# Last pair of batches: the second product of the second MLP in seven block products instead of eight

## The chip, the cores and the metric

One NeuronCore of a Trainium2 chip runs the whole program. The time is the device time of one execution in microseconds; the median of three runs of the kernel before is 1183.4 us (1183.0 to 1185.2).

## The reference

Attention with RMS-normed queries and keys (4 batches, 12 heads, 448 tokens, head size 64), then two MLPs on all 1792 tokens. The second one is what this change touches:

```
h = x @ w_in                       # 1792 x 768  @  768 x 2048
g = h * clip(h + 3, 0, 6) / 6
return g @ w_out                   # 1792 x 2048 @ 2048 x 768
```

## The kernel before

Everything is kept transposed: rows of the weights on the 128 partitions, the 448 tokens of a batch as the moving columns of a matmul. fp32 accuracy comes from splitting each operand into a high part (fp32r) and a low part (the rest), and from three matmuls for each product: high x high, high x low, low x high. A split is one ScalarE copy (the high part) and one subtraction on VectorE or POOL (the low part).

The second MLP works on pairs of batches: the first pair is batches 0 and 1, the last pair 2 and 3. Its work is a list of items (`items`, L1042), each of nine matmuls of 128 x 128 weights on 448 columns. Item i is handled in the main loop (L1219); six items ahead of it (`AHEAD2`) `prepare` (L1065) splits its weights (`halves`, L1004, which gives every second low part to POOL) into one of eight `wt` tiles.

*First product.* Two hidden blocks and two batches are a 2 x 2 block problem (the 768 inner rows are cut in halves), done by Winograd's form of Strassen's algorithm in seven products P1 to P7 instead of eight. The sums of weight blocks (S1 to S4, `temp`, L1078) are made by VectorE, the sums of the inputs beforehand by `xprep` (L1010). Two PSUM banks, sA and sB, take P1 + P6 + P7 + P4 and P2, then P5 + P3; the partial sums on the way are copied out or added (`strassen`, L1174), and the two banks change roles from one group of seven to the next (`swap`). So P2 of a group writes the bank that P4 of the group before has just used. `finish` (L1148) applies the nonlinear step (a ScalarE Relu and a VectorE minimum and product) and, for the pair's first batch, splits the result at once into a `g` tile (`gsplit`, L1143).

*Second product.* For the first batch of the pair, items "L" are woven into the first product's groups, two hidden blocks behind: one item is one hidden block times one half of the 768 outputs, three matmuls into each of three banks; six banks (`acc`) hold the 768 outputs. For the second batch, the hidden blocks wait in `G` tiles in SBUF, and after the groups a sweep of 32 items "M" goes over all of them. So a pair has 32 L items and 32 M items. Then the accumulators are copied out and stored (`out`, L1195).

*Weights.* Each weight tile that an item needs is a numbered use (`uses`, L924). `units` (L943) loads them in order into 12 `wf` tiles, most of them from the DRAM tensor `wfd`, where converted weights were put earlier; a tile is free again after `drop` (L977). All DMAs are issued on SP's queue, in order. Eight `u` tiles of one batch's width serve as temporaries (`utile`, L995).

*Order.* Program order is only a priority: a planner that walks the program with its own cost estimates gives each engine the first instruction that it holds ready, and that order is then fixed. `issue_after` keeps an instruction behind another one on the same engine.

Of the kernel before, what the change touches and what calls it, by code (L numbers as in the profile page):

```python
# [13 lines left out]
F32 = mybir.dt.float32  # L14
F32R = mybir.dt.float32r
# [12 lines left out]
P = 128  # L28
# [23 lines left out]
def fused_kernel(ctx: ExitStack, tc: tile.TileContext, nat, qT, kT, vin, gq, gk,  # L52
# [8 lines left out]
    x2d = dpool.tile([B, KD, P, S], F32, name="x2d")  # L61
    wfd = dpool.tile([2 * M2, P, DM], F32, name="wfd")
    wpd = dpool.tile([KD * M1 // 6, P, 6, 2 * P], F32, name="wpd")

    cpool = ctx.enter_context(tc.tile_pool(name="consts", bufs=1, side="left"))
    pp = ctx.enter_context(tc.tile_pool(name="psum", bufs=2, space=PSUM))
# [23 lines left out]
    def bank(tag, name="bank"):  # L90
        return pp.tile([P, 512], F32, tag=tag, name=name)
# [833 lines left out]
    for p in range(2):  # L925
        for j in range(M2 // 2):
            uses += [("in", 2 * j), ("in", 2 * j + 1)]
            if j:
                uses += [("out", 2 * j - 2), ("out", 2 * j - 1)]
        uses += [("out", M2 - 2), ("out", M2 - 1)]  # L930
        uses += [("out", q) for q in range(M2)]
    fresh = []
    for v, x in enumerate(uses):
        if x not in EARLY and x not in [uses[z] for z in fresh]:
            fresh.append(v)
    dropped = set()

# [5 lines left out]
    def units():  # L943
        n = 0
        for v, (kind, q) in enumerate(uses):
            while v >= NWF and v - NWF not in dropped:
                yield None
            t = mp.tile([P, DM], F32, tag="wf", bufs=NWF, name="wf")
            if v in fresh:
                n += 1  # L950
                load_raw(n)
                r = wr.pop(v)
                if r.dtype == F32:
                    nc.gpsimd.tensor_copy(t, r)
                    yield 0.9
                else:
                    yield from convert(t.bitcast(I32), r)
                yield 0.0
            else:
                dma(t, wfd[q + (M2 if kind == "out" else 0)])  # L960
                yield 0.0
            wf[v] = t

# [9 lines left out]
    def upto(v):  # L973
        while v not in wf:
            assert next(unit) is not None
# [13 lines left out]
    def store(v, t):  # L989
        kind, q = uses[v]  # L990
        dropped.add(v)
        with tc.issue_after(xo["last"].ins):
            dma(wfd[q + (M2 if kind == "out" else 0)], t)

    def utile():  # L995
        return mp.tile([P, S], F32, tag="u", bufs=8, name="u")
# [42 lines left out]

    ORDER = ("P1", "P2", "P6", "L0", "L1", "P5", "P7", "L2", "L3", "P3", "P4")  # L1040
    RIGHT = {"P1": "11", "P2": "21", "P6": "T2", "P5": "T1", "P7": "T3", "P3": "22", "P4": "T4"}
    items = []  # L1042
    base = 0
    for p in range(2):
        prev = None
        for j in range(M2 // 2):
            n = 4 if j else 2
            for z in ORDER:
                if z[0] == "P":
                    items.append((z, p, j, (base, base + 1), z == "P4"))  # L1050
                elif j:
                    h = int(z[1])
                    items.append(("L", p, 2 * j - 2 + h // 2, base + 2 + h // 2, h % 2))
            base += n
        for q in (M2 - 2, M2 - 1):
            for h in range(2):
                items.append(("L", p, q, base + q % 2, h))
        base += 2
        for q in range(M2):
            for h in range(2):  # L1060
                items.append(("M", p, q, base + q, h))
        base += M2
    wt, sx = {}, {}

    def prepare(i):  # L1065
        kind, p, j, v, h = items[i]
        if kind[0] != "P":
            upto(v)
            t = mp.tile([P, 2, NH], F32R, tag="wt", bufs=NWT, name="wt")
            wt[i] = halves(t, wf[v][:, h * NH : h * NH + NH])  # L1070
            if h:
# [23 lines left out]
        wt[i] = halves(t, src)  # L1095
        if h:
            drop(v[0])
            drop(v[1])
# [44 lines left out]
    def gsplit(p, b, q, src):  # L1143
        t = rp.tile([P, 2, S], F32R, tag="g", bufs=4, name="g")
        done[:] = [nc.scalar.activation(t[:, 0, :], src, AF.Copy), nc.vector.tensor_sub(t[:, 1, :], src, t[:, 0, :])]  # L1145
        g[p, b, q] = t

    def finish(p, j, z, src):  # L1148

        b, q = (z % 10 - 1), 2 * j + z // 10 - 1  # L1150
        if b == 0:
            _, u = nonlinear(src, None)
            gsplit(p, 0, q, u)
            return
        if (p, j) not in G:
            G[p, j] = rp.tile([P, 2, S], F32, tag="G", bufs=M2 // 2, name="G")
        nonlinear(src, G[p, j][:, q % 2])

    sA, sB = bank("s", "sA"), bank("s", "sB")
    swap = [(sA, sB)]  # L1160
# [34 lines left out]
    def out(n, t):  # L1195
        o = utile()
        if n % 2:
            nc.vector.tensor_copy(o, acc[n][:, :S])
        else:
            nc.scalar.activation(o, acc[n][:, :S], AF.Copy)  # L1200
        dma(outT[n * P : n * P + P, t * S : t * S + S], o)

    def layer4(i):
        kind, p, q, _, h = items[i]
        b = int(kind == "M")
        w = wt.pop(i)
        x = g[p, b, q] if h == 0 else g.pop((p, b, q))
        for n in range(3 * h, 3 * h + 3):
            if q == 0:
                acc[n] = bank(TAGS[1 + n // 2], "acc")  # L1210
            ns = slice(n % 3 * P, n % 3 * P + P)
            with tc.issue_after(snap["mm"].ins) if (kind, q) == ("L", M2 - 2) else ExitStack():
                mm3(acc[n][:, :S], w[:, 0, ns], w[:, 1, ns], x[:, 0, :], x[:, 1, :], q == 0, q == M2 - 1)
            if q == M2 - 1:
                out(n, PAIRS[p][b])

    prep_to(AHEAD2)
    xg = xrest(0)
    for i, it in enumerate(items):  # L1219
        if i == 4:  # L1220
            xo["last"] = L["last"]
            for e in kept:
                store(*e)
        prep_to(i + AHEAD2)
        kind, p, q = it[:3]
        with ExitStack() as es:
            if kind == "M":
                for z in done:
                    es.enter_context(tc.issue_after(z.ins))
# [12 lines left out]
        (strassen if kind[0] == "P" else layer4)(i)  # L1242
    d1.close()


# [44 lines left out]
```

## Time and profile before

| | |
|---|---|
| runs, median (lowest to highest) | 1183.4 us (1183.0 to 1185.2) |
| profiled execution | 1181.6 us, span 1179.8 us |
| mean granted TensorE clock | 0.994 |
| TensorE matmuls | 1140.6 us busy, 97% of the span, 5627 instructions |
| VectorE, ScalarE, POOL | 72%, 65%, 29% of the span |

The span goes from the first to the last instruction. The second MLP's items begin at about 731 us; the last pair's first product lasts from 954 to 1109 us and its last sweep to 1176 us. Matmuls overlap with the next one, so a busy TensorE says only that it didn't idle; how fast it goes is read from the distance between the starts of its weight loads, one for each matmul.

### The profile page before, as it was taken

How to read it: one execution, taken by the hardware profiler on the slowest of the kernel's cores; microseconds unless marked ns; L12 is line 12 of the kernel's file. 1: busy time of each engine (PE TensorE's matmuls, PEld its weight loads, DVE VectorE, ACT ScalarE, POOL GpSimd, SP SyncE). 2: the span in 40 equal slices, each digit the busy share in tenths (PEclk: the TensorE clock that was granted, in tenths of full speed). 3: DMA queues.
4: the chain of work that ended last, by engine and by line, in shares of the span. 5: the costliest groups of instructions: out<-in, count | busy, mean ns of one | idle time of the engine just before them, and what ended most of it. 6: DMA issues, size and time to landing. Idle time of an engine off the chain costs nothing.

```text
span 1179.8 us, 17400 instructions
## 1 busy us (share of the span) xinstructions
PE 1140.6 (97%) x5627; PEld 973.5 (83%) x5627; DVE 843.7 (72%) x1766; ACT 762.6 (65%) x1603; POOL 340.2 (29%) x297
## 2 busy tenths in 40 slices
PE   5899899999999999999999999999999999999998
PEld 2455576887888888788999999899999999999997
DVE  6778988989788999788883437755547875655542
ACT  6888978897788788877764325555555555454542
POOL 1132323553323223222120004422224542222221
PEclk9899999999999999999999999999999999999999
DMA  8989845788999889988799996522235432222401
GB/s 264 311 284 294 267 153 160 241 279 283 319 309 337 304 284 303 293 296 280 240 321 342 376 334 222 197 81 67 81 89 182 131 125 81 81 81 81 139 16 47
DMA packets 90330, 252.88 MB, mean 214 GB/s; under 512 B 11360, under 2 KB 35936, under 8 KB 90240
## 3 DMA queue, kind: packets, MB, share of 16 engines
q1 hardware_dynamic: 90240, 251.79, 64.6%
q8 instruction: 44, 0.72, 0.2%
q14 instruction: 46, 0.38, 0.1%
HBM read 209.11 MB, written 42.63 MB: 213 GB/s over the span
## 4 chain that ended last, share of the span: by engine, by line
PE 67%; DVE 12%; DMA 10%; ACT 7%; issue 3%; SPq 1%; POOL 0%; ACTq 0%; DVEq 0%; POOLq 0%
PE sA L1170 8%; PE sB L1170 8%; PE bank L392 7%; PE acc L87 7%; PE acc L88 7%; PE acc L86 7%; PE bank L397 4%; PE bank L253 3%; PE bank L654 3%; DVE PP L635 2%; DMA raw<-in_wo_dram 2%; PE bank L86 2%; PE bank L88 2%; PE bank L87 2%; PE bank L628 2%
## 5 line engine op out<-in xcount | busy, mean ns | idle before, releaser
L392 PE MATMUL bank<-xhl,ws 128*128 128x448 f32 x768 | 182.6, 370 | 1.5 <-ACT bs L368 1.2
L392 PEld LDWEIGHTS bank<-xhl,ws 128*128 128x128 f32 x768 | 144.9, 190 | 15.3 <-ACT bs L368 1.5
L647 ACT ACTIVATE PP<-PP,mx 112x448 f32<-112x448 f32 x192 | 127.3, 664 | 41.1 <-DVE mx L642 38.8
L1007 POOL TENSOR_TENSOR wt<-wf,wt 128x384 fp32r<-128x384 f32 x84 | 88.8, 1058 | 207.5 <-ACT wt L1005 201.9
L87 PE MATMUL acc<-g,wt 128*128 128x448 f32 x384 | 141.6, 369 | 0.7 <-DVE g L1145 0.7
L635 DVE CUSTOM_DVE_ANT_0 PP<-bank,rb,rq 112x448 f32<-112x448 f32 x192 | 128.5, 674 | 13.5 <-PE bank L629 11.4
L88 PE MATMUL acc<-g,wt 128*128 128x448 f32 x384 | 136.3, 368 | 0.0
L86 PE MATMUL acc<-g,wt 128*128 128x448 f32 x384 | 127.4, 368 | 0.0
L1005 ACT ACTIVATE wt<-wf 128x384 fp32r<-128x384 f32 x176 | 89.2, 519 | 53.2 <-PE acc L88 34.6
L253 PE MATMUL bank<-woh,w 128*128 128x384 f32 x256 | 99.9, 515 | 14.3 <-DVE woh L152 12.3
L1170 PE MATMUL sA<-xo,wt 128*128 128x448 f32 x504 | 112.0, 366 | 0.0
L1170 PE MATMUL sB<-xo,wt 128*128 128x448 f32 x504 | 111.9, 366 | 0.0
L1007 DVE TENSOR_TENSOR wt<-wf,wt 128x384 fp32r<-128x384 f32 x92 | 65.1, 710 | 52.6 <-ACT wt L1005 49.8
L654 PEld LDWEIGHTS bank<-ident,PP 112*128 112x128 f32 x672 | 78.5, 141 | 29.1 <-issue 7.8
L1170 PEld LDWEIGHTS sA<-xo,wt 128*128 128x128 f32 x504 | 94.5, 188 | 8.5 <-DVE u L1138 0.2
L1170 PEld LDWEIGHTS sB<-xo,wt 128*128 128x128 f32 x504 | 94.7, 188 | 8.2
L663 ACT ACTIVATE xh<-bank 128x448 fp32r<-128x448 f32 (+1 forms) x156 | 82.6, 537 | 25.8 <-PE bank L654 21.4
L673 DVE TENSOR_TENSOR xl<-bank,xh 128x448 fp32r<-128x448 f32 x142 | 86.9, 615 | 17.0 <-ACT xh L663 16.0
L654 PE MATMUL bank<-ident,PP 112*128 112x112 f32 x672 | 94.0, 261 | 4.3 <-DVE xl L673 2.0
L149 DVE SCALAR_TENSOR_TENSOR raw<-raw 128x384 int32<-128x384 int32 (+1 forms) x112 | 69.4, 620 | 37.2 <-ACT raw L147 32.8
L397 PE MATMUL bank<-xhl,ws 128*128 128x448 f32 x384 | 94.7, 366 | 0.0
L146 ACT ACTIVATE raw<-raw 128x384 f32<-128x384 f32 (+1 forms) x112 | 63.7, 568 | 37.6 <-DMA raw<-in_wo_dram 15.6
(138 smaller groups left out, 2438.7 us busy)
## 6 DMA issues: line engine op xcount, KB each, us to landing
ws<-w12d SPq DMA_DIRECT2D x48, 768.0 KB
wf<-wfd SPq DMA_DIRECT2D x88, 384.0 KB
ws<-wpd SPq DMA_DIRECT2D x32, 768.0 KB
raw<-in_wo_dram SPq DMA_DIRECT2D x44, 384.0 KB
raw<-in_w_dram SPq DMA_DIRECT2D x32, 384.0 KB
w12d<-ws SPq DMA_DIRECT2D x16, 768.0 KB
qr<-in_qT_dram SPq DMA_DIRECT2D x24, 448.0 KB
kr<-in_kT_dram SPq DMA_DIRECT2D x24, 448.0 KB
```

Source lines behind the costliest of these rows:

```text
L86: nc.tensor.matmul(ps, lh, rh, start=first, stop=False)
L87: nc.tensor.matmul(ps, lh, rl, start=False, stop=False)
L88: return nc.tensor.matmul(ps, ll, rh, start=False, stop=last)
L253: nc.tensor.matmul(ps[:, :NH], W["w3"][a, c // 4][:, cs], W["woh"][c, n], start=c == 0, stop=c == M1 - 1)
L392: nc.tensor.matmul(ps[:, :S], w[:, 0, ks], x[:, y, :], start=k == 0 and y == 0, stop=False)
L397: nc.tensor.matmul(ps[:, :S], w[:, 1, ks], L["xhl"][i][:, 0, :], start=False, stop=k == KD - 1)
L635: anchors[8 * i + s].append(nc.vector.tensor_tensor_reduce(out=T["PP", i][:, c, sl], in0=ps[:CP, :S], in1=T["rb", i][:, sl], op0=ALU.mult, ...
L647: anchors[8 * i + s].append(nc.scalar.activation(v, v, AF.Exp, bias=T["m", i][:, 8 + s : 9 + s], accum_out=T["sum", i][:, s : s + 1]))
L654: nc.tensor.transpose(ps[:, c * CP : c * CP + CP], src[:, c, kb * P : kb * P + P], ident[:CP, :CP])
L1005: nc.scalar.activation(t[:, 0, :], src, AF.Copy)
L1007: (nc.vector if nsplit[0] % 2 else nc.gpsimd).tensor_sub(t[:, 1, :], src, t[:, 0, :])
L1170: mm = nc.tensor.matmul(ps[:, :S], w[:, a, ks], x[:, c, :], start=first and k == 0 and n == 0, stop=k == KD // 2 - 1 and n == 2, skip_grou ...
```

## The change

In the last pair the second product becomes a 2 x 2 block problem too: two hidden blocks by two batches, times the two halves of the outputs, in Winograd's seven products. The items are now "O" with a number 1 to 7, each with one weight block of 384 columns and one operand of 448 columns, again nine matmuls, three to a bank.

- Products 1 and 2 (plain blocks, first batch) stand in the groups of the first product, one or two groups behind. They sum to the first block of the result.
- The other five need all hidden blocks and run after the groups, in passes over the eight block pairs: 6 (on top of product 1's banks) woven with 5, then 7 (on top of 6) woven with 3 (on top of 5), then 4 (on top of 7). Between passes the accumulators are copied out or added to.
- The sums of w_out blocks are made in the first pair by `combos` when its L items are prepared, and stored to the DRAM tensor `sd`; in the last pair they are loaded through `uses` as "s12" and "s34". Tiles of `out` rows are therefore kept until the second of two.
- The sums of hidden blocks are made in the last pair's groups by `three` and `fourth`, stored to `td` and `t4d`, loaded back by `tload` and split by `tsplit` two items ahead.
- In the last pair, and in the first pair's sweep, all low parts are made by VectorE.

The core of the diff (declarations and the spelled-out first-pair items are left out):

```diff
...
+            uses += [("s12", j) for j in range(M2 // 2)] + [("s34", j) for j in range(M2 // 2)]
+            uses += [("out", 2 * j + 1) for j in range(M2 // 2)]
...
-    def halves(t, src):
+    def halves(t, src, alone=False):
         nc.scalar.activation(t[:, 0, :], src, AF.Copy)
         nsplit[0] += 1
-        (nc.vector if nsplit[0] % 2 else nc.gpsimd).tensor_sub(t[:, 1, :], src, t[:, 0, :])
+        (nc.vector if nsplit[0] % 2 or alone else nc.gpsimd).tensor_sub(t[:, 1, :], src, t[:, 0, :])
...
+    for j in range(NJ):
+        for z in ("P1", "P2", "O2", "P6", "P5", "P7", "P3", "O1", "P4"):
+            if z[0] == "P":
+                items.append((z, 1, j, (group[j], group[j] + 1), z == "P4"))
+            elif z == "O1" and j >= 1:
+                items.append(("O", 1, j - 1, group[j] + 2, "1"))
+            elif z == "O2" and j >= 2:
+                items.append(("O", 1, j - 2, group[j - 1] + 3, "2"))
+    last = group[NJ]
+    items += [("O", 1, NJ - 1, last, "1"), ("O", 1, NJ - 2, group[NJ - 1] + 3, "2")]
+    base = last + 2
+    first_o = len(items)
+    sets = (("6", base), ("7", base + NJ), ("4", base + 2 * NJ)), (("5", base), ("3", base + NJ))
+    top, low = ([("O", 1, j, v + j, z) for z, v in x for j in range(NJ)] for x in sets)
+    for n in range(0, len(top), NJ):
+        up, dn = top[n : n + NJ], low[n : n + NJ]
+        items += up[:2]
+        if n == 0:
+            items.insert(-1, ("O", 1, NJ - 1, last + 1, "2"))
+        for z in range(2, NJ):
+            items += dn[z - 2 : z - 1] + [up[z]]
+        items += dn[-2:]
...
+    def combos(j, w1, w2):
+        a11, a21 = w1[:, :NH], w1[:, NH:]
+        a12, a22 = w2[:, :NH], w2[:, NH:]
+        s = []
+        for n, op in enumerate((ALU.add, ALU.subtract, ALU.subtract, ALU.subtract)):
+            s.append(utile()[:, :NH])
+            x, y = ((a21, a22), (s[0], a11), (a11, a21), (a12, s[min(n, 1)]))[n]
+            nc.vector.tensor_tensor(out=s[n], in0=x, in1=y, op=op)
+            dma(sd[j, n // 2, :, n % 2], s[n])
...
+    def three(j):
+        a = X["a"] = rp.tile([P, 2, S], F32, tag="G", bufs=M2 // 2, name="G")
+        b = X["b"]
+        nc.vector.tensor_sub(a[:, 0], X[12], X[11])
+        nc.vector.tensor_sub(a[:, 1], b[:, 1], a[:, 0])
+        nc.vector.tensor_sub(b[:, 0], b[:, 1], X[12])
+        dma(td[j, 0], a)
+        dma(td[j, 1], b)
+
+    def fourth(j):
+        t = utile()
+        nc.vector.tensor_sub(t, X[21], X["a"][:, 1])
+        dma(t4d[j // 2, :, j % 2], t)
...
+    def tload(n):
+        while len(tl) < min(n, len(plan)):
+            d, j, z = plan[len(tl)]
+            t = rp.tile([P, 2, S], F32, tag="G", bufs=M2 // 2, name="G")
+            dma(t, d[j] if z is None else d[j, z])
+            tl[len(tl)] = t
...
+    def outer(i):
+        _, p, j, _, h = items[i]
...
+        low = 3 * (h in "253")
...
+        first, end = j == 0 and h in "1253", j == NJ - 1
+        for n in range(3):
+            ps, ns = acc[low + n][:, :S], slice(n * P, n * P + P)
+            with tc.issue_after(snap["mm"].ins) if i >= first_o - 2 else ExitStack():
+                for a, (y, z) in enumerate(((0, 0), (0, 1), (1, 0))):
+                    nc.tensor.matmul(ps, w[:, y, ns], x[:, z, :], start=first and a == 0, stop=end and a == 2,
+                                     skip_group_check=h in "674")
...
+        if i >= first_o - 6:
+            tload((i - first_o) // 2 + 4)
+        tsplit(i + 2)
+        now[0] = i
+        (strassen if kind[0] == "P" else outer if kind == "O" else layer4)(i)
+        while wait and wait[0][0] <= i:
+            with tc.issue_after(done[1].ins):
+                wait.pop(0)[1]()
```

## Rows read from the trace of the kernel before

**Rows 1.** The page, part 1: busy time, share of the span, instructions.
```profile
PE 1140.6 (97%) x5627; PEld 973.5 (83%) x5627; DVE 843.7 (72%) x1766; ACT 762.6 (65%) x1603; POOL 340.2 (29%) x297
```

**Rows 2.** Busy time by stretch: stretch, length, engines with counts, clock, DMA share, GB/s.
```profile
760.00:880.00 120.00, 120.00 (x588) 110.13 (x587) 69.43 (x108) 61.70 (x120) 32.78 (x32) 1.00 0.27 80
900.00:950.00 50.00, 50.00 (x243) 45.48 (x243) 45.23 (x52) 28.39 (x61) 30.40 (x24) 1.00 0.44 138
960.00:1100.00 140.00, 140.00 (x687) 128.53 (x686) 78.90 (x128) 72.84 (x140) 38.76 (x38) 1.00 0.27 80
1120.00:1170.00 50.00, 50.00 (x244) 45.48 (x243) 19.51 (x24) 17.99 (x36) 12.26 (x12) 1.00 0.05 16
```

**Rows 3.** Waits of TensorE, 720 to 1180 us: total, times, longest.
```profile
PE acc L87 <- DVE g L1145: 0.7, 1, 0.7
```

**Rows 4.** Weight loads in order of time, last sweep: start, us, what; 18 lie between.
```profile
1140.00 0.19 PEld L87 LDWEIGHTS acc<-g,wt 128*128 128x128 f32 x1
...
1143.93 0.19 PEld L88 LDWEIGHTS acc<-g,wt 128*128 128x128 f32 x1
```

**Rows 5.** The same, first group of the last pair.
```profile
954.17 1.81 PEld L1170 LDWEIGHTS sA<-xo,wt 128*128 128x128 f32 x9
955.99 1.81 PEld L1170 LDWEIGHTS sB<-xo,wt 128*128 128x128 f32 x9
...
963.29 0.60 PEld L86 LDWEIGHTS acc<-g,wt 128*128 128x128 f32 x3
...
965.14 1.84 PEld L1170 LDWEIGHTS sB<-xo,wt 128*128 128x128 f32 x9
```

**Rows 6.** Single lines, 960 to 1180 us: count, duration in ns (shortest/median/longest).
```profile
L1007 POOL TENSOR_TENSOR wt<-wf,wt x42: 1009/1021/1197, 962.9 to 1161.9; 128x384 fp32r<-128x384 f32 x42
L1007 DVE TENSOR_TENSOR wt<-wf,wt x41: 541/558/1062, 961.1 to 1160.0; 128x384 fp32r<-128x384 f32 x41
L1080 DVE TENSOR_TENSOR sx<-wf,sx x7: 544/558/559, 964.9 to 1086.4; 128x384 f32<-128x384 f32 x7
L1190 DVE TENSOR_TENSOR u<-sA,u x12: 609/618/625, 963.8 to 1107.6; 128x448 f32<-128x448 f32 x12
L1145 DVE TENSOR_TENSOR g<-G,g x16: 611/1082/1084, 1111.7 to 1162.4; 128x448 fp32r<-128x448 f32 x16
L1005 ACT ACTIVATE wt<-wf x83: 508/524/528, 960.5 to 1161.3; 128x384 fp32r<-128x384 f32 x83
```

**Rows 7.** VectorE in order of time, two neighbours: start, us, what.
```profile
922.24 0.61 DVE L1028 TENSOR_TENSOR wr<-u 128x448 f32<-128x448 f32 x1
922.77 0.61 DVE L1007 TENSOR_TENSOR xo<-u,xo 128x448 fp32r<-128x448 f32 x1
```

**Rows 8.** In order of time: P4 of a group, and VectorE's last read of its bank.
```profile
988.48 2.02 PE L1170 MATMUL sB<-xo,wt 128*128 128x448 f32 x9
...
991.21 0.62 DVE L1138 SCALAR_TENSOR_TENSOR u<-u,sB 128x448 f32<-128x448 f32 x1 [2.16 <-ACT u L1137]
```

**Rows 9.** DMA view: GB/s in 40 slices, 1100 to 1104 us; total, 738 to 745.
```profile
GB/s 0 0 0 0 0 0 0 0 0 0 0 0 0 0 215 246 154 184 92 154 276 215 215 461 461 461 338 184 123 123 31 0 0 0 0 0 0 0 0 0
...
DMA packets 911, 2.49 MB, mean 355 GB/s; under 512 B 100, under 2 KB 104, under 8 KB 911
```

**Rows 10.** SP's queue in order of time: the issue of the load in rows 9.
```profile
1100.48 0.32 SPq L97 DMA_DIRECT2D wf<-wfd  x1
```

**Rows 11.** Waits of SP's queue, 730 to 1180 us: total, times, longest.
```profile
SPq L97 <- DVE wt L1007: 230.1, 55, 8.5
```

**Rows 12.** The last instruction, in order of time.
```profile
1176.16 0.63 DVE L1198 COPY u<-acc 128x448 f32<-128x448 f32 x1 [0.61 <-PE acc L88]
```

**Rows 13.** Groups by line, VectorE, 966 to 1088 us: count, busy us, mean ns.
```profile
L1007 DVE TENSOR_TENSOR wt<-wf,wt 128x384 fp32r<-128x384 f32 x21 | 13.1, 624 | 17.1 <-ACT wt L1005 16.9
L1145 DVE TENSOR_TENSOR g<-u,g 128x448 fp32r<-128x448 f32 x12 | 10.1, 840 | 6.1 <-ACT g L1145 6.1
L1080 DVE TENSOR_TENSOR sx<-wf 128x384 f32<-128x384 f32 x12 | 9.5, 788 | 0.1
```

More of the change, by code (lines that the diff above doesn't have):

```diff
@@ L959, in units @@
             else:
-                dma(t, wfd[q + (M2 if kind == "out" else 0)])
+                dma(t, home(kind, q))
                 yield 0.0
@@ L992, in store @@
         with tc.issue_after(xo["last"].ins):
-            dma(wfd[q + (M2 if kind == "out" else 0)], t)
+            dma(home(kind, q), t)
     def utile():
@@ L1041, in fused_kernel @@
     RIGHT = {"P1": "11", "P2": "21", "P6": "T2", "P5": "T1", "P7": "T3", "P3": "22", "P4": "T4"}
+    NJ = M2 // 2
     items = []
     base = 0
[L1044 to L1062, printed above, removed]
@@ L1063, in fused_kernel @@
-    wt, sx = {}, {}
+    for j in range(NJ):
+        for z in ORDER:
+            if z[0] == "P":
+                items.append((z, 0, j, (base, base + 1), z == "P4"))
+            elif j:
+                h = int(z[1])
+                items.append(("L", 0, 2 * j - 2 + h // 2, base + 2 + h // 2, h % 2))
+        base += 4 if j else 2
+    for q in (M2 - 2, M2 - 1):
+        for h in range(2):
+            items.append(("L", 0, q, base + q % 2, h))
+    base += 2
+    for q in range(M2):
+        for h in range(2):
+            items.append(("M", 0, q, base + q, h))
@@ L1065, in prepare @@
+    wt, sx = {}, {}
+    def combos(j, w1, w2):
[7 more added lines that the diff above has]
+            dma(sd[j, n // 2, :, n % 2], s[n])
     def prepare(i):
         kind, p, j, v, h = items[i]
+        if kind == "O":
+            upto(v)
+            c = slice(NH, 2 * NH) if h in "634" else slice(0, NH)
+            wt[i] = halves(mp.tile([P, 2, NH], F32R, tag="wt", bufs=NWT, name="wt"), wf[v][:, c], True)
+            if h not in "67":
+                drop(v)
+            return
@@ L1094, in prepare @@
         t = mp.tile([P, 2, NH], F32R, tag="wt", bufs=NWT, name="wt")
-        wt[i] = halves(t, src)
+        wt[i] = halves(t, src, p == 1)
         if h:
@@ L1153, in finish @@
             gsplit(p, 0, q, u)
+            if p == 1:
+                X[z] = u
+                if z == 21:
+                    wait.append((now[0] + 2, partial(fourth, j)))
             return
-        if (p, j) not in G:
-            G[p, j] = rp.tile([P, 2, S], F32, tag="G", bufs=M2 // 2, name="G")
-        nonlinear(src, G[p, j][:, q % 2])
+        if p == 0:
+            if (p, j) not in G:
+                G[p, j] = rp.tile([P, 2, S], F32, tag="G", bufs=M2 // 2, name="G")
+            nonlinear(src, G[p, j][:, q % 2])
+        elif z == 22:
+            X["b"] = rp.tile([P, 2, S], F32, tag="G", bufs=M2 // 2, name="G")
+            nonlinear(src, X["b"][:, 1])
+        else:
+            _, X[z] = nonlinear(src, None)
+            wait.append((now[0] + 2, partial(three, j)))
+    X, wait = {}, []
+    def three(j):
[10 more added lines that the diff above has]
+        dma(t4d[j // 2, :, j % 2], t)
     sA, sB = bank("s", "sA"), bank("s", "sB")
@@ L1215, in layer4, with tsplit @@
                 out(n, PAIRS[p][b])
+                if kind == "M":
+                    acc.pop(n)
+    plan = [(td, j, 0) for j in range(NJ)] + [(td, j, 1) for j in range(NJ)] + [(t4d, j, None) for j in range(NJ // 2)]
+    tl = {}
+    def tload(n):
[4 more added lines that the diff above has]
+            tl[len(tl)] = t
+    def tsplit(i):
+        if first_o <= i < len(items) and items[i][4] not in "12":
+            j, h = items[i][2], items[i][4]
+            if h == "4":
+                src = tl[2 * NJ + j // 2][:, j % 2]
+            else:
+                src = tl[j + NJ * (h in "73")][:, int(h in "63")]
+            gsplit(1, h, j, src)
@@ new lines, in outer, with put @@
+    def outer(i):
+        _, p, j, _, h = items[i]
+        if not acc:
+            for n in range(KD):
+                acc[n] = bank(TAGS[1 + n // 2], "acc")
+        low = 3 * (h in "253")
+        w = wt.pop(i)
+        x = g.pop((1, 0, 2 * j + int(h) - 1) if h in "12" else (1, h, j))
+        first, end = j == 0 and h in "1253", j == NJ - 1
[5 more added lines that the diff above has]
+                                     skip_group_check=h in "674")
+        if not end:
+            return
+        b1, b2 = PAIRS[1]
+        def put(n, b, t):
+            dma(outT[n * P : n * P + P, b * S : b * S + S], t)
+        for n in range(3):
+            ps = acc[low + n][:, :S]
+            if h == "1":
+                snap["c", n] = utile()
+                nc.scalar.activation(snap["c", n], ps, AF.Copy)
+            elif h == "2":
+                t = snap["c", n]
+                nc.vector.tensor_add(t, ps, t)
+                put(n, b1, t)
+            elif h == "6":
+                snap["o", n] = xtile("22", n).bitcast(F32)
+                nc.scalar.activation(snap["o", n][:, 1], ps, AF.Copy)
+            elif h == "5":
+                t = snap["o", n]
+                nc.scalar.activation(t[:, 0], ps, AF.Copy)
+                nc.vector.tensor_add(t[:, 1], ps, t[:, 1])
+            elif h == "4":
+                t = utile()
+                if n % 2:
+                    nc.vector.tensor_copy(t, ps)
+                else:
+                    nc.scalar.activation(t, ps, AF.Copy)
+                put(n + 3, b1, t)
+            else:
+                t = utile()
+                nc.vector.tensor_add(t, ps, snap["o", n][:, int(h == "3")])
+                put(n + 3 * (h == "7"), b2, t)
```

26 lines of the change are left out of this document (21 added, 5 removed).

## The prediction

> **What bounds the kernel now.** I read the views in this order: busy time of the engines, busy time by stretch, TensorE's waits, weight loads in order of time, single instructions by line, and the DMA view. TensorE is busy 97% of the span [rows 1]. In the second MLP it is busy in every microsecond of four stretches between 760 and 1170 us, at a granted clock of 1.00 [rows 2], and from 720 us on its whole wait for other engines is 0.7 us [rows 3]. So in this part the time is the number of matmuls times their spacing. The other engines have room: VectorE is busy 69.4 of 120 us in the first product of the first pair, 78.9 of 140 in that of the last pair, 19.5 of 50 in the last sweep; only between 900 and 950 us (second sweep of the first pair, with the operands of the last pair being made) is it nearly full, 45.2 of 50. The DMA engines carry 80 GB/s there [rows 2].
>
> **What goes.** The last pair's second product is 64 items of 9 matmuls (16 hidden blocks, 2 halves, 2 batches); with 7 products for 8 block rows it is 56. 8 x 9 = 72 matmuls go. In the last sweep, whose matmuls also change bank after every three, weight loads start 3.93 us apart over 19 steps, 0.2068 us each [rows 4]: 72 x 0.2068 = 14.9 us. The 56 new items have the same form (three matmuls to a bank), so I leave them at that; items of the first product, nine matmuls to one bank, start 1.82 to 1.83 us apart, 0.203 per matmul [rows 5]. If the new ones ran at that, 504 x 0.0038 = 1.9 us more would go; that is the lower bound.
>
> **What comes in the last pair's first product.** A group of 7 first-product items and 2 second-product items (from the third group on) lasts 7 x 1.83 + 2 x 1.86 = 16.5 us on TensorE, where 7 + 4 items took 20.3 before. VectorE per group: 9 low halves (all of them now, POOL took every second one) and 4 weight sums, 13 at 0.558; 3 additions, 4 nonlinear steps, 2 splits, and 4 new subtractions of hidden blocks, 13 at about 0.62 [rows 6]: 7.3 + 8.1 = 15.3 us of 16.5, 93%. But back to back such an instruction starts 0.53 us after the one before while its own row says 0.61 [rows 7]; with 0.08 taken off each, 26 instructions hold the engine for 13.3 us, 80%. [...]
>
> The tightest place: P4 leaves its bank through a ScalarE and a VectorE instruction, and P2 of the next group clears that bank with only P1 in between. P4 starts at 988.48, the bank is free at 991.21 + 0.62 = 991.83 [rows 8], P2 could start at 988.48 + 2 x 1.83 = 992.14: 0.3 us are left. The one VectorE instruction that may be running takes up to 0.62, so in a bad group 0.3 us is lost; but the planner put second-product matmuls into such gaps, and from the third group on it has O2 for that. I count nothing there; 8 x 0.6 = 4.8 us is the upper end.
>
> The first group has no second-product items at all. Before, the planner pulled some forward there: after five first-product items, at 963.29, nine matmuls of the second product stood in until P3 at 965.14 [rows 5]; I read that as P3's weights, which hang on three sums in a row, coming late. Nothing stands in for them in the new group 0, and VectorE has 24 instructions in 12.8 us: I count this gap, 1.85 us, as lost. It may be nothing, since the low halves no longer wait 1.02 us on POOL and POOL no longer slows VectorE there; with the same again in the second group it is 3.7.
>
> **What comes in the first pair.** Eight times, four weight sums (8 x 4 x 0.56 = 18 us of VectorE) and four stores of 192 KB. They lie beside matmuls in a stretch where VectorE is 58% busy [rows 2]; 2.2 us more per 20 make 69%. Tiles of `out` rows are kept two items longer. In the second sweep all low halves go to VectorE: 32 x 0.56 = 18 us instead of 9, but a split lasts 1.08 us instead of 0.61 (median and shortest of the last sweep) where a 1.02 us POOL subtraction runs beside it [rows 6], and POOL now does few. VectorE does not get fuller than the 45.2 of 50 that cost TensorE nothing. Cost zero; without that cover, the rival below. The four temporaries share eight `u` slots.
>
> **The three passes.** 40 items of 1.86 us, 74.4 us. Each needs a weight split and an operand split: VectorE 0.56 + 0.61 = 1.17, ScalarE 0.52 and, at 448 columns for 384, some 0.6, 1.1 us of 1.86 [rows 6]: hidden. Accumulators that are read and used on have one item (1.86 us) or more between last write and next use; a read takes 0.62, three follow the matmuls at their pace: hidden. In passes one and two (59.5 us) 12 weight tiles of 384 KB and 16 operand tiles of 448 KB are loaded, 12.1 MB, 203 GB/s; over 7 us the queue carried 355 GB/s [rows 9], and the loads are issued four items (7.4 us) ahead of their split, weights up to 12 tiles ahead. On SP's queue 16 + 8 stores of hidden sums now stand between loads of the last pair; its first product asks 165 GB/s instead of 80. A store waits for a VectorE instruction at most a few us, the weight loads behind it have tiles in hand: zero.
>
> The tail stays: three accumulators, a copy each, and stores. The last copy was VectorE's at 1176.16, 0.63 us [rows 12], and becomes ScalarE's, 0.54: -0.1.
>
> **Sum**, against the profiled execution (1181.6 us, 1.8 above the span): 1181.6 - 14.9 - 0.1 + 1.9 = 1168.5. The median of the runs, 1183.4, is 1.8 above that execution: 1170.3 us.
>
> **Rivals.**
> (A) VectorE becomes the bound of the last pair's first product. If its instructions keep the means they have there now, POOL's part in it: low halves 0.62, sums 0.79 for two and 0.55 for two, splits and new subtractions 0.84, the other seven 0.62 [rows 6, 13]. A group: 9 x 0.62 + 2.7 + 6 x 0.84 + 7 x 0.62 = 17.6 us; eight groups less three missing low halves 138.9, against 126.7 of TensorE: 12.2 us lost, 1180.6. For it: the count. Against it: the means are so high because of POOL, which is idle in this stretch afterwards, and rows 7. Part of it is likelier than all: 1174 to 1181.
> (B) Slower: the loads pace passes one and two. A single 384 KB load is issued at 1100.48 and its last bytes move some 2.6 us later (40 slices of 0.1 us from 1100.0) [rows 9, 10]; 448 KB takes 2.8. If each load is issued only when the one before has landed, because the slot it waits for is freed by work on that one, then 12 x 2.6 + 16 x 2.8 = 76.0 us instead of 59.5: 16.5 lost, 1186.8. It decides from 28 loads at about 2.6 us each. For it: SP works in order, and its loads already wait 4.2 us each for a VectorE split (230.1 us, 55 times) [rows 11]. Against it: those waits are for free slots far ahead of need, and loads overlap wherever the queue is full (355 GB/s). [...]
> (C) The sums in the first pair take the `u` tiles: four of eight are held until their stores land, 2.6 us if a store is like that load [rows 9, 10], and TensorE, which waits for a copy into such a tile, has 1.83 us of cover: 8 x 0.8 = 6.4 lost, 1176.7. Against it: only three or four other tiles live at that point.
> That the change doesn't do what it says: the matmul count is fixed by the item list, so this is not open; only idle time is.
>
> **How the numbers follow.** Two tenths of a per cent, 2.4 us, is what a measurement here can tell. Forecast (1166.5 to 1174): 0.64, faster. A: 0.15, faster but for the 0.02 in which it costs a microsecond more. C: 0.09, faster. B: 0.08, slower. Anything else: 0.04, of it 0.01 faster, 0.02 same, 0.01 slower. Faster 0.64 + 0.13 + 0.09 + 0.01 = 0.87, same 0.04, slower 0.09. Range: from the lower bound (no idle time, new items at 0.203: 1183.4 - 14.9 - 1.9 - 0.1 = 1166.5) to 1178, which takes in C and half of A; B, the other half of A and the rest are left out, 0.2.
>
> **What would show it.** TensorE's instructions fall by 72; the new outer items stand 1.86 us apart; TensorE waits under 3 us in the last pair, most of it in its first two groups. VectorE busy 85 to 95% there with instructions at 0.56 and 0.61, POOL almost idle. A shows as VectorE at 95% or more and TensorE waiting for weights or banks group after group; B as waits for DMA on the operand splits of the passes; C as waits for `u` tiles between 750 and 890 us. The prediction is wrong if TensorE idles more than 6 us from 720 us on, or if the new items are spaced other than 0.20 to 0.21 us.

## The result and the profile after

The changed kernel takes 1167.94 us, the median of four runs (1163.84 to 1169.3), against 1183.2 us of the kernel before in the same comparison: ratio 0.9865, 95% interval 0.9835 to 0.9896. The prediction was 1170.3 us, in a range of 1166.5 to 1178. The profiled execution took 1169.3 us, its span is 1167.5 us, the mean granted clock 0.994 as before.

The page's first part, and the busy time by stretch (length, then TensorE, weight loads, VectorE, ScalarE, POOL with their counts, clock, DMA share, GB/s); the stretches stand where those of [rows 2] stood, and the last one lies in the passes:

```profile
PE 1126.6 (96%) x5555; PEld 960.2 (82%) x5555; DVE 898.8 (77%) x1929; ACT 773.8 (66%) x1624; POOL 261.8 (22%) x221
```

```profile
763.00:883.00 120.00, 120.00 (x588) 110.13 (x587) 80.33 (x133) 61.68 (x120) 32.79 (x32) 1.00 0.36 116
903.00:953.00 50.00, 50.00 (x244) 45.48 (x243) 43.90 (x68) 28.87 (x61) 17.82 (x11) 1.00 0.45 141
963.00:1090.00 127.00, 127.00 (x624) 116.87 (x623) 103.03 (x197) 75.08 (x145) 0.00 (x0) 1.00 0.53 176
1095.00:1160.00 65.00, 65.00 (x316) 59.12 (x316) 41.30 (x76) 34.70 (x70) 0.00 (x0) 1.00 0.54 204
```

72 TensorE instructions are gone [rows 1], and TensorE is still busy in every microsecond of the four stretches, with the same number of instructions per microsecond (588 in 120 us before and after). The room was paid by the others: VectorE 80.33 of 120 us for 69.43, and 103.03 of 127 (81%) in the last pair's first product, the DMA engines 116 to 204 GB/s for 16 to 138 [rows 2]. POOL does nothing from 963 us on.

Waits of TensorE after 720 us (total, times, longest): one row, the one of [rows 3] under a new line number.

```profile
PE acc L90 <- DVE g L1200: 0.7, 1, 0.7
```

So the time of the second MLP is read best from its first and its last weight load. The kernel before (start, us, what):

```profile
731.52 1.81 PEld L1170 LDWEIGHTS sA<-xo,wt 128*128 128x128 f32 x9
...
1175.55 0.19 PEld L88 LDWEIGHTS acc<-g,wt 128*128 128x128 f32 x1
```

After; the row at 1163.02 holds three loads, the last of which starts 0.60 - 0.19 = 0.41 us later. Between them, the seven first-product items of the last pair's first group, and 23 loads in the passes:

```profile
734.36 1.81 PEld L1252 LDWEIGHTS sA<-xo,wt 128*128 128x128 f32 x9
...
957.03 1.81 PEld L1252 LDWEIGHTS sA<-xo,wt 128*128 128x128 f32 x9
958.85 1.81 PEld L1252 LDWEIGHTS sB<-xo,wt 128*128 128x128 f32 x9
...
964.33 1.80 PEld L1252 LDWEIGHTS sA<-xo,wt 128*128 128x128 f32 x9
966.15 1.83 PEld L1252 LDWEIGHTS sB<-xo,wt 128*128 128x128 f32 x9
...
1139.88 4.74 PEld L1333 LDWEIGHTS acc<-g,wt 128*128 128x128 f32 x23
...
1163.02 0.60 PEld L1333 LDWEIGHTS acc<-g,wt 128*128 128x128 f32 x3
```

From first to last: 1175.55 - 731.52 = 444.03 us before, 1163.43 - 734.36 = 429.07 us after, 14.96 us less. This execution started its second MLP 2.84 us later than that of the kernel before, with the same 3467 weight loads ahead of it; that lateness is in its 1169.3 us, and the first experiments ask whether it belongs to the change. "Length" below is always first to last weight load of the second MLP.

Single lines of VectorE in the last pair (count, shortest/median/longest in ns), beside [rows 6]: low halves, hidden sums, and the subtractions of the operand splits.

```profile
L1020 DVE TENSOR_TENSOR wt<-wf,wt x75: 549/553/561, 969.6 to 1151.1; 128x384 fp32r<-128x384 f32 x75
L1230 DVE TENSOR_TENSOR G<-u x8: 617/619/623, 972.8 to 1087.1; 128x448 f32<-128x448 f32 x8
L1200 DVE TENSOR_TENSOR g<-G,g x40: 615/625/626, 1088.2 to 1157.2; 128x448 fp32r<-128x448 f32 x40
```

The durations above 1 us (up to 1062 ns for a low half, 1082 in the median for a split before) are gone, and so is POOL's part. The last instruction is now a ScalarE copy, as [rows 12] was VectorE's:

```profile
1164.04 0.54 ACT L1363 ACTIVATE u<-acc 128x448 f32<-128x448 f32 x1 [0.69 <-PE acc L1333]
```

### The profile page after: what moved, and what is told of

It reads as the page before. It is cut to its first block, busy times and chain, and to the rows that moved or that the text cites. A ratio compares the mean times of both kernels' runs of the same rounds, so it can differ in the third digit from the quotient of the medians.

```text
span 1167.5 us, 17553 instructions
## 1 busy us (share of the span) xinstructions
PE 1126.6 (96%) x5555; PEld 960.2 (82%) x5555; DVE 898.8 (77%) x1929; ACT 773.8 (66%) x1624; POOL 261.8 (22%) x221
## 4 chain that ended last, share of the span: by engine, by line
PE 70%; DVE 12%; DMA 8%; ACT 7%; issue 3%; SPq 0%; POOL 0%; ACTq 0%; DVEq 0%; POOLq 0%
PE acc L1333 9%; PE sA L1252 8%; PE bank L395 8%; PE sB L1252 8%; PE bank L400 4%; PE bank L256 4%; PE bank L657 3%; PE acc L90 3%; PE acc L91 3%; PE acc L89 3%; DVE PP L638 2%; DMA raw<-in_wo_dram 2%; PE bank L89 2%; PE bank L91 2%; PE bank L90 2%
## 5 line engine op out<-in xcount | busy, mean ns | idle before, releaser
L1333 PE MATMUL acc<-g,wt 128*128 128x448 f32 x504 | 108.4, 369 | 0.0
L1018 ACT ACTIVATE wt<-wf 128x384 fp32r<-128x384 f32 x168 | 84.7, 517 | 28.3 <-PE acc L91 9.7
L1333 PEld LDWEIGHTS acc<-g,wt 128*128 128x128 f32 x504 | 94.7, 188 | 9.2
L1020 DVE TENSOR_TENSOR wt<-wf,wt 128x384 fp32r<-128x384 f32 x143 | 87.1, 619 | 18.0 <-ACT wt L1018 17.8
L631 PE MATMUL bank<-K,Q 128*112 128x448 f32 x192 | 80.4, 420 | 6.7 <-DVE mx L638 6.4
L256 PEld LDWEIGHTS bank<-woh,w 128*128 128x128 f32 x256 | 49.5, 200 | 44.6 <-DVE woh L155 16.0
```

Source lines behind the costliest of these rows:

```text
L256: nc.tensor.matmul(ps[:, :NH], W["w3"][a, c // 4][:, cs], W["woh"][c, n], start=c == 0, stop=c == M1 - 1)
L1020: (nc.vector if nsplit[0] % 2 or alone else nc.gpsimd).tensor_sub(t[:, 1, :], src, t[:, 0, :])
L1333: nc.tensor.matmul(ps, w[:, y, ns], x[:, z, :], start=first and a == 0, stop=end and a == 2, skip_group_check=h in "674")
```

## The experiments

**Unaltered kernels again.** Is the late start part of the change?

> The changed kernel once more, unaltered. Theory 1 (only the 72 matmuls count, nothing in the second MLP waits for anything new): 14.9 to 15.0 us less than before in the median, ratio about 0.9873, and in its trace 429.6 us or so from the first matmul of the second MLP to the last one, as in the first trace of it; the start of that part may lie anywhere in 730 to 735 us, since it is the part ahead of it that varies. Theory 2 (the change also costs 2 to 3 us ahead of the second MLP, where its first matmul came at 734.4 instead of 731.5 us): the first matmul is late by 2 to 3 us again, and the median gain stays at 12 to 13 us.

> The kernel before, unaltered, for a second trace. If the time ahead of the second MLP varies by itself, its first matmul does not stand at 731.5 us again but anywhere within some 3 us of it, while from there to the last matmul it is 444.6 us again. If that part is fixed for a kernel, it stands at 731.5 within 0.5 us.

The changed kernel again: 1169.62 us (1167.04 to 1175.44), ratio 0.9876 (0.9836 to 0.9917). One execution of the kernel before: 1183.85 us. Their first weight loads, of the changed kernel and of the one before:

```profile
732.09 1.81 PEld L1252 LDWEIGHTS sA<-xo,wt 128*128 128x128 f32 x9
```

```profile
733.77 1.81 PEld L1170 LDWEIGHTS sA<-xo,wt 128*128 128x128 f32 x9
```

The lengths came out at 429.07 and 444.03 us, the same to 0.01 us as in the first pair of traces, while the starts changed places. So the late start is not of the change. Over all traces of this study the start lies between 729.1 and 737.9 us; the runs of one kernel scatter by about that, and the length is the sharper measure.

**The costs counted at zero, one at a time.** The sums in the first pair alone, put into the kernel before (it writes `sd` and nothing reads it):

```diff
...
-            if h:
+            if h and (kind == "M" or p == 1):
+                drop(v)
+            elif h and j % 2:
+                combos(j // 2, wf[v - 1], wf[v])
+                drop(v - 1)
                 drop(v)
```

> The kernel before, with one part of the change alone: the sums of w_out blocks are made in the first pair and stored, and nobody reads them; tiles of out rows are kept until the second of two. Theory 1: within 2 us of the kernel before, TensorE waits for nothing new. Rival C: four of the eight temporaries are held for a store of 2.6 us, eight times, and up to 6 us are lost between 750 and 890 us.

1183.06 us, ratio 0.9991 (0.9972 to 1.0009), length 444.07. They cost nothing, and rival C falls for this change.

Every second low half back on POOL, in the last pair and in the first pair's sweep:

```diff
-        (nc.vector if nsplit[0] % 2 or alone else nc.gpsimd).tensor_sub(...)
+        (nc.vector if nsplit[0] % 2 else nc.gpsimd).tensor_sub(...)
```

> POOL takes every second low half again, in the first pair's sweep and in the last pair, as before the change. Theory 1: VectorE then has some 4.5 instructions less in a group of the last pair but meets POOL again, so its splits last up to 1.08 us; it does not get full and TensorE waits for nothing: within 2.4 us of the changed kernel. Rival: the low halves on VectorE alone are what keeps TensorE fed; then groups of the last pair and the passes show waits of TensorE for weights, 5 us or more in all.

1169.57 us, ratio 0.9873 (0.9819 to 0.9927), length 430.05: 1.0 us more than the changed kernel. Taking POOL out is worth a microsecond and no more. What POOL does to VectorE shows in six groups of the last pair (the changed kernel's row of the same stretch stands below):

```profile
974.00:1073.00 99.00, 99.00 (x483) 89.89 (x482) 78.00 (x125) 54.48 (x107) 29.36 (x27) 1.00 0.49 162
```

With POOL at work VectorE is busy 78.00 us with 125 instructions, without it 79.92 with 154, 0.62 and 0.52 us each: the subtractions that POOL took over saved VectorE almost nothing.

Hidden sums loaded two items ahead instead of four:

```diff
-            tload((i - first_o) // 2 + 4)
+            tload((i - first_o) // 2 + 2)
```

> The changed kernel with each load of stored hidden sums issued two tiles later, in the same step as its split instead of four items ahead. A load takes 2.6 to 2.8 us from issue to its last byte and the split 1.2 us, together 4.0, and TensorE needs the operand two items (3.7 us) later. Theory 1: at most some 0.3 us is short for each of 16 tiles and most are covered by the order of other work, so 0 to 5 us lost: the four items of lead are cover, not need. Rival B (the loads pace the passes): the lead is needed, and 10 us or more are lost.

1172.88 us, ratio 0.9906 (0.9878 to 0.9934), length 434.49, 5.4 more, a little over the 0 to 5 of theory 1 and far from rival B's 10. All of it is lost as pass one begins. Its waits of TensorE, and its busy time by stretch there:

```profile
PE acc L1333 <- ACT g L1200: 3.3, 2, 2.2
```

```profile
1085.00:1092.00 7.00, 3.65 (x17) 2.69 (x16) 6.49 (x14) 3.08 (x7) 0.00 (x0) 0.99 0.93 313
1092.00:1095.00 3.00, 3.00 (x9) 2.65 (x9) 1.08 (x2) 0.45 (x1) 0.00 (x0) 0.50 1.03 419
1095.00:1100.00 5.00, 5.00 (x25) 4.54 (x24) 2.39 (x5) 2.80 (x6) 0.00 (x0) 0.97 1.04 407
```

The waits are 3.3 us; about 1.1 us of the rest is in the second row. After this wait of 2.2 us the granted clock is 0.50 for some 3 us, and nine matmuls fit where 14.5 do at 0.2068. After the start the loads keep up even so: rival B's pacing isn't there, at up to 419 GB/s, twice the 204 of the changed kernel's passes. Here four items of lead are enough (no wait for these loads), two are not (3.3 us).

**How full may VectorE be?** One subtraction of `three` repeated 4 and 10 times more in each group of the last pair:

```diff
+        for _ in range(5):        # 11 in the second kernel
-        nc.vector.tensor_sub(a[:, 0], X[12], X[11])
+            nc.vector.tensor_sub(a[:, 0], X[12], X[11])
```

> One of the new subtractions of hidden blocks is repeated four times in each of the last pair's eight groups (448 columns each). Theory 1 (an instruction holds VectorE for the 0.53 us between two starts, so a group holds it 13.3 us of 16.5): 13.3 + 2.1 = 15.4 us fit, under 2 us lost. Rival (it holds VectorE for the 0.61 us of its row, so a group holds it 15.3 us): 15.3 + 2.5 = 17.8 us, 1.3 us more than TensorE's 16.5 in each group, some 10 us lost.

> The same subtraction repeated ten times in each group. Theory 1 (0.53 us each): 13.3 + 5.3 = 18.6 us against 16.5, 2.1 us more than TensorE needs, times eight 17 us lost, some less for the slack that is there at the start. Rival (0.61 us each): 15.3 + 6.1 = 21.4, 4.9 us a group, 39 us lost. If nothing is lost, VectorE's load says nothing here at all.

With 4 more: 1173.02 us, ratio 0.9896 (0.9866 to 0.9927), length 434.53, 5.5 more; with 10 more: 1195.1 us, ratio 1.0099 (1.0077 to 1.0122), length 455.14, 26.1 more. Neither theory has the 5.5 (under 2, or some 10). Of the 26.1, 4.5 are one wait in the passes, for a load of hidden sums, and some 1.4 the clock behind it (0.58 for 3.7 us, 11 matmuls). That leaves about 20 for the groups, nearer to the 17 of theory 1 than to the rival's 39. With 10 VectorE is the bound of the groups; stretch of about three groups, and VectorE in order of time:

```profile
1003.00:1061.00 58.00, 50.47 (x241) 44.55 (x240) 56.12 (x108) 27.84 (x54) 0.00 (x0) 1.00 0.42 137
```

```profile
1019.53 0.55 DVE L1135 TENSOR_TENSOR sx<-wf,sx 128x384 f32<-128x384 f32 x1
1020.00 0.62 DVE L1231 TENSOR_TENSOR G<-u 128x448 f32<-128x448 f32 x1
1020.53 0.55 DVE L1135 TENSOR_TENSOR sx<-wf 128x384 f32<-128x384 f32 x1
1021.00 0.62 DVE L1231 TENSOR_TENSOR G<-u 128x448 f32<-128x448 f32 x1
```

108 instructions in 58 us are 0.54 us each: the next one starts 0.47 us after one of 384 columns and 0.53 after one of 448, while their own rows say 0.55 and 0.62. By the rows' durations the 36 instructions of a group (26 and 10) would take 36 x 0.59 = 21.2 us; the groups took 19.55. That is the spacing of [rows 7], now in an engine that is really full. But with 4 more, 30 x 0.54 = 16.2 us still fit into 16.5, and 5.5 us were lost. Where: waits of TensorE, then ScalarE, then TensorE in order of time (bracket: idle time before, and what ended it).

```profile
PE sA L1253 <- ACT u L1265: 3.3, 3, 1.1
PE sB L1253 <- ACT u L1265: 1.0, 1, 1.0
```

```profile
996.73 1.19 ACT L1018 ACTIVATE wt<-sx 128x384 fp32r<-128x384 f32 x2 [1.54 <-PE sB L1253]
997.83 0.53 ACT L1265 ACTIVATE u<-sA 128x448 f32<-128x448 f32 x1
```

```profile
991.64 1.99 PE L1253 MATMUL sA<-xo,wt 128*128 128x448 f32 x9
...
998.41 2.10 PE L1253 MATMUL sA<-xo,wt 128*128 128x448 f32 x9 [1.10 <-ACT u L1265]
```

The same place in the changed kernel, on ScalarE:

```profile
995.00 0.53 ACT L1264 ACTIVATE u<-sA 128x448 f32<-128x448 f32 x1
...
997.67 0.93 ACT L1018 ACTIVATE wt<-sx 128x384 fp32r<-128x384 f32 x2
```

P6's product in sA ended at 991.64 + 1.99 = 993.63. In the changed kernel the same product started at 992.08 and ended some 1.99 us later, at 994.07; its copy ("snapshot") runs at 995.00, 0.9 us after it. In the kernel with 4 more, two weight copies stand ahead of it in ScalarE's fixed order; they read nothing from TensorE, so what they wait for until 996.73 is a `wt` tile that a matmul still reads, with ScalarE idle 1.54 us. The snapshot runs at 997.83, 4.2 us after its product, and the next product for that bank waits 1.10 us. This order stands in every second group (three of them), and so do three of the four gaps; the fourth, 1.04 us, is in the last group, where one weight copy stands ahead. The four gaps are 4.3 us of the 5.5; at the one shown the weight loads stop for 1.48 us where the matmul waits 1.10. The stretch of six groups, in this kernel and in the changed one:

```profile
974.00:1073.00 99.00, 95.68 (x467) 87.11 (x466) 88.65 (x172) 54.22 (x103) 0.00 (x0) 1.00 0.48 158
```

```profile
974.00:1073.00 99.00, 99.00 (x487) 91.20 (x486) 79.92 (x154) 56.20 (x109) 0.00 (x0) 1.00 0.50 165
```

VectorE is 90% busy instead of 81%, and not full in the stretch that loses.

**The change in both pairs.** It would remove 72 more matmuls, with more work for VectorE per group in the first pair as well. The core of the edit; the items of both pairs are written by the last pair's lines.

```diff
-        if p == 0:
-            uses += [("out", q) for q in range(M2)]
-        else:
-            uses += [("s12", j) for j in range(M2 // 2)] + ...
+        uses += [("s12", j) for j in range(M2 // 2)] + ...
...
+    for p in range(2):
+        group = [base + 4 * j - 2 * (j > 0) for j in range(NJ + 1)]
+        for j in range(NJ):
+            for z in ("P1", "P2", "O2", "P6", "P5", "P7", "P3", "O1", "P4"):
...
+            if p == 0 and h == "1":
+                upto(v + 1)
+                combos(j, wf[v], wf[v + 1])
```

> The same seven products for the first pair too: its L and M items (64) become 56 O items, the sums of w_out blocks are made and stored when product 1 is prepared, the operands of the last pair are made during the first pair's passes, and all low halves of weights go to VectorE. Theory 1 (the matmul count sets the time): 72 more matmuls go, 14.9 us less than the changed kernel, 29.8 less than before. Rival: in the first pair's groups VectorE has four weight sums more, 13.3 + 1.9 = 15.2 us of 16.5 by the spacing of starts and 17.6 by the rows' durations, and meets POOL at its start; then up to 8 us of the 14.9 are lost there again.

1167.86 us (1164.6 to 1171.74), ratio 0.9868 (0.9842 to 0.9894), length 426.85: of the 14.9 us only 2.2 came, and the 12.7 that did not are more than the 8 of the rival. Waits of TensorE:

```profile
PE sA L1237 <- ACT u L1249: 4.4, 4, 1.8
PE sB L1237 <- ACT u L1249: 3.7, 4, 1.1
PE sA L1237 <- DVE u L1257: 2.6, 1, 2.6
PE acc L1318 <- ACT g L1190: 1.4, 1, 1.4
PE sB L1237 <- DVE u L1257: 0.6, 1, 0.6
```

The same snapshots, once in each group of the first pair. Three theories were left: too few `u` tiles for the snapshots, the order on ScalarE, VectorE itself. First the tiles: one fewer in the changed kernel, and, in the other two, the hidden blocks written straight into their `G` tiles and summed in place, so that they hold no `u` tile (with four more subtractions, the second one of `three` is then the one repeated).

```diff
-        return mp.tile([P, S], F32, tag="u", bufs=8, name="u")
+        return mp.tile([P, S], F32, tag="u", bufs=7, name="u")
```

```diff
...
-            _, X[z] = nonlinear(src, None)
-            wait.append((now[0] + 2, partial(three, j)))
+            nonlinear(src, X["b"][:, 0])
+            wait.append((now[0] + 2, partial(three, j, X["a"], X["b"])))
...
-        nc.vector.tensor_sub(a[:, 0], X[12], X[11])
+        nc.vector.tensor_sub(a[:, 0], b[:, 0], a[:, 0])
```

> The changed kernel with seven u tiles instead of eight, nothing else. Theory u: waits for ScalarE copies appear in the last pair's groups, 1 to 2 us each in most groups, 5 to 15 us in all, though VectorE has not one instruction more. Rival V: under 2 us.

> The kernel with seven products in both pairs, with one difference: two hidden blocks of a group (products P2 and P3) are kept where their sums go (halves of G tiles, subtracted in place) instead of in u tiles until the sums are made. Same matmuls, same instructions on VectorE. In that kernel TensorE waited 12.7 us, 8.1 of it for ScalarE copies into u tiles. Theory u (the eight u tiles run out: the copies have no free tile, and TensorE waits for the copies): these waits go, the second MLP takes 414 to 419 us instead of 426.9, and the time falls to 1154 to 1160. Rival V (VectorE, 31 instructions in a group of 16.5 us, is simply too full): the second MLP stays at 424 us or more, and the time within 3 us of 1168.

> The changed kernel with four extra subtractions in each group of the last pair, as before, and the two hidden blocks kept in place. The extra subtractions alone cost 5.5 us from the first matmul of the second MLP to the last (434.5 for 429.1), four waits of 1.4 us for ScalarE copies. Theory u: 429 to 431 us, the same VectorE load costs nothing. Rival V: 433 us or more.

One tile fewer: 1169.73 us, ratio 0.9893 (0.9854 to 0.9931), length 429.10, nothing lost. In place: both pairs 1168.51 us, 0.9874 (0.9846 to 0.9903), length 430.02 for 426.85; four more subtractions 1174.51 us, 0.991 (0.9878 to 0.9941), length 434.22 for 434.53. In place, TensorE's waits for the copies in the kernel with both pairs are:

```profile
PE sA L1236 <- ACT u L1248: 4.5, 4, 1.2
PE sB L1236 <- ACT u L1248: 4.4, 4, 1.1
```

8.9 us for 8.1, and with four more subtractions 4.4 for 4.3. So the theory of the tiles falls for the gaps of the groups. Rival V's numbers came, but the next run takes its reason away. (Most of the 3.2 us by which the length grew is the clock; see the last section.) Then the order, in the kernel with both pairs: each weight copy stands behind the last snapshot before it in the program.

```diff
-        nc.scalar.activation(t[:, 0, :], src, AF.Copy)
+        with tc.issue_after(copied[0].ins) if alone and copied else ExitStack():
+            nc.scalar.activation(t[:, 0, :], src, AF.Copy)
...
-            nc.scalar.activation(snap[kind], r, AF.Copy)
+            copied[:] = [nc.scalar.activation(snap[kind], r, AF.Copy)]
```

> Seven products in both pairs, as in the run that had both, and one change of order: each ScalarE copy of a weight block (the high part) is held behind the last copy of a partial sum (the snapshots of P1, P6 and P5) that stands before it in the program. In the run with both pairs, in every second group of the first pair, two weight copies stood ahead of the snapshot of P6, and waited with it for the same matmul. Theory (the order on ScalarE costs the gaps): the once-a-group gaps of 0.8 to 1.5 us in the first pair go, and with them most of 12.7 us; second MLP 416 to 420 us after 426.85, ratio to the kernel before 0.977 to 0.981, 1156 to 1161 us. Rival 1 (VectorE, 88% busy in that stretch, is what sets the pace; the order on ScalarE only shows it): the waits move to VectorE's additions, second MLP 425 to 428 us, ratio 0.985 to 0.988. Rival 2 (weight copies held back come late): TensorE waits for weights instead, second MLP over 429 us, ratio above 0.99.

1162.89 us (1158.55 to 1166.43), ratio 0.9824 (0.979 to 0.9857), length 421.93: 4.9 shorter than with both pairs, just short of what the theory expected, and by its length outside both rivals (the interval of the ratio alone still touches rival 1). The groups of the first pair in the kernel with both, then in this one, and the largest waits that this one has left:

```profile
765.00:863.00 98.00, 92.93 (x448) 83.86 (x449) 85.87 (x165) 52.60 (x100) 0.00 (x0) 1.00 0.55 191
```

```profile
765.00:863.00 98.00, 98.00 (x480) 89.72 (x479) 87.47 (x173) 52.59 (x107) 0.00 (x0) 1.00 0.59 201
```

```profile
PE sA L1238 <- ACT u L1250: 2.2, 1, 2.2
PE acc L1319 <- ACT g L1191: 2.0, 2, 1.6
PE sA L1238 <- DVE u L1258: 1.4, 1, 1.4
PE sB L1238 <- DVE u L1258: 0.9, 1, 0.9
```

TensorE is busy in all of 98.00 us, where it was in 92.93, with VectorE at 89% instead of 88%. So in these groups it was the order on ScalarE, and here a VectorE at nine tenths loses nothing by itself. What is left are single waits at both ends of the first pair's groups (2.7 us before 765, 4.2 between 863 and 890). The longest of them, 2.2 us, does come from a `u` tile:

```profile
867.03 0.54 ACT L1250 ACTIVATE u<-sA 128x448 f32<-128x448 f32 x1 [4.05 <-DMA sd<-u]
```

Eight weight sums stand back to back there, and the last snapshot waits for a tile until the store of a sum to `sd` has landed. That is rival C's mechanism, once and not eight times, and in a kernel that makes more of its sums at once; the kernel with both pairs waits 1.8 us at that place. Whether this is faster than the changed kernel isn't settled by the runs: the intervals 0.979 to 0.9857 and 0.9835 to 0.9896 overlap, and this profile's second MLP began latest of all, at 737.89. Its length says 7.1 us. Not tried: the same order in the kernel with four more subtractions, and why the planner sets the copies ahead in some groups only.

## Why the prediction was right

**72 matmuls.** The term was 14.9 us; the length fell by 14.96, twice. New items at the old spacing: 22 steps in 4.74 - 0.19 = 4.55 us are 0.2068 us each, and the lower bound of 0.203 didn't come.

**The first group of the last pair: mis-sized.** The step "I count this gap, 1.85 us, as lost" failed. From 957.03 on the seven items follow each other 1.82 to 1.86 us apart, and P3 starts at 966.15, 1.82 us after the item before it. The nine matmuls of [rows 5] were read as a sign that P3's weights come late; nothing of the kind is late in the changed kernel, so an instruction that stands in a place shows no wait by itself. (Whether they would have been late before, beside POOL, no run asked.) With zero for it the sum is 1183.4 - 14.9 - 0.1 = 1168.4, between the medians 1167.94 and 1169.62 of the changed kernel. The runs alone could not have told that from 1170.3: the interval 0.9835 to 0.9896 is 7 us wide, so the 2.4 us that the prediction called measurable was too fine, and it is the lengths in the traces that decide.

**VectorE.** The forecast was 26 instructions and 80% of a group by spacing, 93% by durations. It was 154 in 99 us, 25.7 to a group, and 79.92 us, 81%. The line "85 to 95%" in what would show it was too high: it belonged to the durations that the sum had just rejected. Rival A priced at durations; its 17.6 us a group would need 33 instructions at the 0.54 us that ten more subtractions showed, seven more than there are. The other half of rival A, POOL's part in the durations, went with POOL: 0.52 us for each instruction in the groups, 0.62 with POOL back. The run with VectorE at 97% shows again that here a duration isn't occupancy: the rows say 0.55 and 0.62 us, and the next instruction starts after 0.47 and 0.53.

**The tight place of P2** cost nothing in all eight groups (no wait in the list). What the prediction didn't see is what broke first when VectorE was filled up: not its own throughput but a snapshot in ScalarE's order. Four more instructions per group were enough. That the order is the cause was shown by changing it in the kernel with both pairs; in the kernel with four more it is read from the trace.

**Loads and sums at zero.** Both right: no wait for a DMA, 444.07 us with the sums alone. (The 80 GB/s that the prediction gives as the traffic is that of the two first products; between 900 and 950 us it was 138 [rows 2]. The 2.8 us that it gives a load of 448 KB came: one that stands alone in the changed kernel is issued at 1129.97 and moves its last bytes between 1132.7 and 1132.8.) The lead of four items has under two in reserve; rival B was right about the direction of that risk, but its price is that of a start (5.4 us), not of every load. **Tail:** span after the last instruction's end 3.0 us before, 1167.5 - 1164.58 = 2.9 after.

## What to carry to other kernels

Where TensorE waited 0.7 us in all, 72 removed matmuls came back one for one, and a spacing read from 20 weight loads predicted it to a tenth of a microsecond (14.9 us for 14.96); measure such a change between two marks inside the trace, not over the whole run, when what lies before scatters by several times what you ask. Price an engine's room by the distance between the starts of neighbours, not by durations (VectorE here: 0.47 and 0.53 us, for durations of 0.55 and 0.62). When a stage is nearly full, look at what stands ahead of a bank's copy in the order of its engine: here a copy that waited 1.54 us for a free tile held up one that didn't, and TensorE waited 1.10 us for that one. And where two lengths differ by a few microseconds, read the granted clock before looking for a cause in the kernel (2.4 of the 3.2 us of the in-place kernel).

## What the runs showed of the hardware

The granted clock after a wait. In the kernel with both pairs and the snapshots first, a product waited 2.2 us for a snapshot; busy time by stretch around it:

```profile
867.30:871.10 3.80, 3.47 (x10) 3.10 (x11) 2.93 (x7) 3.03 (x8) 0.00 (x0) 0.61 0.90 276
871.10:876.00 4.90, 4.90 (x24) 4.49 (x23) 3.61 (x8) 3.92 (x9) 0.00 (x0) 0.95 0.68 231
```

After it the mean clock is 0.61 for 3.8 us, and ten matmuls take its 3.47 busy us, where 17 would go at 0.2068, as in the late loads above (0.50 after 2.2 us). The waits of 1.1 us in the kernel with four more subtractions left it at 1.00 (974 to 1073).

But after a wait of 2.6 us it was lower in one kernel and not in another. In the kernel with both pairs TensorE waits 2.6 us for VectorE in the first group of the first pair, and so it does with the hidden blocks in place. The stretch right after that wait, in the one and in the other:

```profile
751.70:755.00 3.30, 3.30 (x16) 3.04 (x17) 3.30 (x7) 2.39 (x4) 0.00 (x0) 1.00 0.55 216
```

```profile
745.80:749.50 3.70, 3.68 (x10) 3.30 (x11) 3.44 (x7) 1.34 (x2) 0.00 (x0) 0.50 0.58 224
```

In the first the clock stays at 1.00. In the second it is 0.50, and still 0.72 in the next 4.5 us: 28 matmuls in 8.2 us, some 2.4 us more than they take at 0.2068. That is most of the 3.2 us by which the in-place kernel is longer. In both TensorE was busy without a break for the 10 us up to the wait; what decides between the two isn't shown. A wait of 1.8 us in the kernel with both pairs (868 to 880) left the clock at 1.00, too, so no run shows that the 1.85 us gap, which I priced at its own length, would have cost more by the clock.
